# Warm-up products cut shorter at equal columns, and one quad's loads moved along VectorE's queue

## The chip, the cores and the metric

The kernel runs on one core of a Trainium2 chip. The metric is the device time of one execution in microseconds (us). A core has five engines that work side by side, each through its own queue in order: TensorE (PE, with its weight loads shown apart as PEld), VectorE (DVE), ScalarE (ACT), GpSimd (POOL) and SyncE (SP). SyncE only issues transfers here; GpSimd and, at the start, ScalarE issue some too.

## The reference

Attention over 8 batches of 12 heads, 448 positions and 64 dimensions, with q and k normalised first, and then a dense layer with a GELU between two weight matrices.

```
q_n = q / sqrt(mean(q*q) + 1e-6) * g_q          # k likewise with g_k
attn = softmax(q_n @ k_n.T / 8)
x = (attn @ v), heads side by side               # (3584, 768)
out = gelu_tanh(x @ w_in) @ w_out                # w_in (768, 2048), w_out (2048, 768)
```

## The kernel before

**Tiling.** A batch's 12 heads are taken as three quads `c` of four heads. For each quad, q and k are loaded (`load`, line 118, 448 KB each), squared (`square`), summed (`total`), turned into inverse roots (`rsqrt`), multiplied (`normed`) and transposed, so that positions lie along the free axis. Scores are made in 21 units per batch (three quads by seven tiles of positions, `unit`, line 327), each 128 by 896; ScalarE takes the exponential of each (`exp`, line 338) out of one of a few PSUM buffers. `products` (line 369) multiplies the exponentials with ones, for the sums, and with v. The result, divided, is xT (`quad_x`). The first layer (`mm1_turn`, line 521) and the second one (`quartered`, line 473) follow; the second layer of one batch is run in between the attention of the next.

**The order of the work** is written out by hand. Nothing reorders it: what a function emits goes to its engine's queue at that place. Three parts matter.

- The *front*: lines 739 to 896. The first loads go out on SyncE and ScalarE, GpSimd clears and loads the small vectors, and TensorE gets products that nobody reads: `idle(n, w)` (line 266) emits n products of a 128x128 block of ones with 448 columns of ones, into a PSUM tile that is overwritten later. Sixteen stand at the very start (line 802), one ahead of the first scores (line 844), and two at a time behind each of the first five units of batch 0 (the list `mid`, lines 857 to 862). `mid` gives, for each unit's number, what is emitted after its exponential; `first_attention` (line 705) runs it. With only two PSUM buffers for scores here, a unit can't begin before the exponential two units back has read its buffer.
- *Batch 1's attention*: `attention` (line 582) with the tables `SECOND` (line 575). One string gives TensorE's order (steps of the second layer, units, products), another VectorE's: words such as A0, B0, F0, G0 (sums of exponentials), T, R, S (turning and spreading the reciprocals), M (the division into xT). Words L0, L1, K0 and a0 to a5 have no work of their own; each runs the functions that the list `extra` (lines 929 to 948) holds for it, in the order in which they were put in. a0 is there for `total` of batch 2's first quad's q, a1 for its k.
- *Late loads*: `late_loads(b, c)` (line 138) first writes one element of the tile that is to be loaded, on VectorE, and then issues the load on SyncE. The load must wait for that write, so VectorE's place in its queue sets when the transfer is asked for. At L1, behind G0, stand the loads of batch 2's second and third quads, at L0 those of its first. Batch 3's first quad is asked for in the same way ahead of unit 14. The third quad's squares are taken by ScalarE at the end of batch 1's attention (line 675), after the last exponential.

SyncE's queue holds, from batch 1's attention on, loads, stores of results (`store`, line 450) and transfers that transpose (`dma_trans`, line 314), in the order of emission.

Of the kernel before, what the change touches and what calls it, by code (L numbers as in the profile page):

```python
# [17 lines left out]
def kernel(  # L18
# [174 lines left out]
    def rsqrt(b, c=slice(0, NCH), ns=both, near=(), ts=slice(0, NT), twice=False):  # L193

        if b not in rinvs:
            rinvs[b] = smp.tile([P, NCH, 2, 2, NT], F32, tag="rinv", name="rinv")
        lg = smp.tile([P, NCH, 2, 2, NT], F32, tag="lg", name="lg")
        nc.scalar.activation(
            lg[:, c, ns, :, ts], sss[b][:, c, ns, :, ts], AF.Ln, scale=1.0 / D, bias=eps
        )  # L200

        def to_sbuf(far):
            if far:
                ns = slice(far[0], far[-1] + 1)
                nc.scalar.activation(rinvs[b][:, c, ns], lg[:, c, ns], AF.Exp, scale=-0.5)  # L205

        if twice:
            to_sbuf(near)
        if near:
            if ts.start == 0:  # L210
                place(b, c)
            if len(near) == 2:
                t = roots["qk", b, c]
                nc.scalar.activation(t, lg[:, c], AF.Exp, scale=-0.5)
            else:
                t = roots["qk"[near[0]], b, c]
                nc.scalar.activation(t[:, :, ts], lg[:, c, near[0], :, ts], AF.Exp, scale=-0.5)
        to_sbuf([n for n in range(2)[ns] if n not in near])
# [44 lines left out]
                y if i < 2 else dst, z, 1.5, y, op0=ALU.add, op1=ALU.mult  # L263
            )

    def idle(n, w):

        for _ in range(n):
            nc.tensor.matmul(w, filler[:, :128], filler, start=True, stop=True)

    def normed(b, c, n, eng, ts=slice(0, NT)):
        if (n, b, c) not in nrms:
            nrms[n, b, c] = nrmp.tile([P, NT, 2, D], BF16, tag=f"nrm{n}", name=f"nrm{n}")
        m = ts.stop - ts.start
        root = rinvs[b][:, seat(b, c), "qk".index(n)] if eng is nc.gpsimd else roots[n, b, c]
        eng.tensor_mul(  # L276
            nrms[n, b, c][:, ts].rearrange("p t a d -> p a t d"),
            raws[n, b, c][:, :, ts],
            root[:, :, ts].to_broadcast([P, 2, m, D]),
        )  # L280
# [505 lines left out]
    def warm():  # L786
        return oall[0][:, :S]
# [11 lines left out]
    for h in range(2):  # L799
        nc.gpsimd.tensor_mul(gprod[h * D:(h + 1) * D], grow[:, 0], grow[:, 1])  # L800
    nc.gpsimd.tensor_mul(gbf, grow[:, 0], grow[:, 1])
    idle(16, warm())
    for a in range(2):
        square(0, 0, "q", nc.scalar, slice(a, a + 1))
        total(0, 0, "q", slice(a, a + 1))
# [47 lines left out]
    def turn_new(c, ts):  # L853
        tps["k"] = ps_m.tile([128, 1024], BF16, tag="mm", name="tp")
        turn(0, c, "k", ts)

    mid = [(0, lambda: idle(2, warm())),
           (1, lambda: turn_new(0, t_rest), lambda: idle(2, warm())),
           (2, lambda: rsqrt(0, 1, near=(0, 1)), lambda: idle(2, warm())),
           (3, lambda: put(0, 0, "k", t_rest), lambda: normed(0, 1, "q", nc.vector),  # L860
            lambda: normed(0, 1, "k", nc.vector, t_first), lambda: idle(2, warm())),
           (4, lambda: idle(2, warm())),
           (5, lambda: turn(0, 1, "q"), lambda: put(0, 1, "q"),
            lambda: turn_new(1, t_first), lambda: put(0, 1, "k", t_first)),
           (6, lambda: total(0, 2, "q"), lambda: total(0, 2, "k")),
# [50 lines left out]
    for b in range(B):  # L916
        m1, side, extra, ends = [], [], [], []
        if b == 0:

            m1 = [(0, lambda: total(1, 0, "k"),  # L920
                   lambda: total(1, 2, "q"), lambda: total(1, 2, "k"),
                   lambda: rsqrt_newton(1), lambda: normed_both(1, 2, nc.gpsimd),
                   lambda: normed(1, 0, "k", nc.gpsimd)),
                  (2, lambda: total(1, 1, "q"), lambda: total(1, 1, "k"),
                   lambda: normed(1, 0, "q", nc.vector), lambda: rsqrt_last(1),
                   lambda: normed_both(1, 1, nc.vector)),
                  (6, lambda: trans(1, 0, nc.scalar), lambda: late_transposed(1, 2)),
                  (7, lambda: trans(1, 1))]
            extra += [("L0", lambda: late_loads(2, 0)),
                      ("L1", lambda: late_loads(2, 1), lambda: late_loads(2, 2)),  # L930
                      ("K0", lambda: gain(1, 2))]

            for n in "qk":
                sqs[n, 2, 1] = [
                    nrmp.tile([P, NT, 2, D], BF16, tag=f"nrm{m}", name="sq")
                    .rearrange("p t a d -> p (t a d)").bitcast(F32)
                    .rearrange("p (a t d) -> p a t d", a=1, t=NT) for m in "qk"
                ]

            extra.append(("K0", lambda: gpsimd_waits(kT[:1, 2, 0, 0, :1])))  # L940
            at = 0
            for c in range(2):
                for n in "qk":
                    for hs in (slice(0, 1), slice(1, 2)) if c else (both,):
                        extra += [
                            ("K0", lambda c=c, n=n, hs=hs: square(2, c, n, nc.gpsimd, hs)),
                            (f"a{at}", lambda c=c, n=n, hs=hs: total(2, c, n, hs))]
                        at += 1
        elif b + 1 < B:

            m1.append((0, lambda: gpsimd_waits(ess[b, NCH - 1][:1, 0, 0, :1])))
            for c in range(NCH):
                if b == 1 and c + 1 == NCH:
                    m1 += [(0, lambda: total(2, 2, "q")), (0, lambda: total(2, 2, "k")),
                           (0, lambda: rsqrt_last(2))]
                m1 += [(0, lambda c=c: normed_both(b + 1, c, nc.gpsimd)),
                       (4 * c + 4, lambda c=c: transposed(b + 1, c))]
            m1 += [(9, lambda: gain(b + 1, 0)), (14, lambda: gain(b + 1, 1))]
        if 0 < b and b + 2 < B:
            m1 += [(4, lambda: loads(b + 2, 1)), (8, lambda: loads(b + 2, 2))]  # L960
            for c, at in ((0, 4), (1, 9)):
                for i, (n, a) in enumerate((n, a) for n in "qk" for a in range(2)):
                    m1.append((at + i, lambda c=c, n=n, a=a: squared(b + 2, c, n, a)))
                m1 += [(at + 2, lambda c=c: total(b + 2, c, "q")),
                       (at + 4, lambda c=c: total(b + 2, c, "k"))]
            for n in "qk":
                m1.append((13, lambda n=n: square(b + 2, 2, n, nc.gpsimd)))
                extra.append(("first", lambda n=n: total(b + 2, 2, n)))
        if 0 < b and b + 1 < B:
            extra.append(("first", lambda: gain(b + 1, 2)))  # L970
        m1 = plan(*m1)
        for f in range(nf // 2 if b == 0 else nf):
            i, part = f // 4 * 2, f % 4
            if b == 0:
                if f == 2:
                    mm1(0, 5)
                    square(1, 1, "k", nc.scalar)
                elif f > 2:
                    mm1_pair(f)
            elif f == 1:  # L980
                mm1_turn(b, 0, 1, late)
                mm1_turn(b, 1, 1, late)
                mm1_turn(b, 0, 0, late, end=True)
            elif f == 3:
                mm1_turn(b, 1, 0, late, end=True)
            elif part == 1:
                mm1_turn(b, i, 0, range(HP), begin=True)
                mm1_turn(b, i + 1, 0, range(HP), begin=True)
                mm1_turn(b, i, 1, range(HP), end=True)
            elif part == 3:  # L990
                mm1_turn(b, i + 1, 1, range(HP), end=True)
            for fn in m1.get(f, ()):
                fn()
        if b + 1 == B:
            final(b)
            break
        nc.scalar.preload_act_table_set(EXP_SET)
        if b + 2 < B:
            ends.append(lambda: rsqrt(b + 2, slice(0, NCH if b else NCH - 1)))
            side += [(0 if b else 11, lambda: load_v(b + 2, 0, HP))]  # L1000
            if b + 3 < B:
                side.append((3, lambda: loads(b + 3, 0)) if b else (14, lambda: late_loads(3, 0)))
        if b == 0:
            start.close()
            ps_x = ctx.enter_context(
                tc.tile_pool(name="ps_x", bufs=1, space=bass.MemoryType.PSUM))
            for i in (2, 3):
                rounds.append(ps_x.tile([128, 2, 512], F32, tag=f"t{i}", name=f"t{i}"))
            late_on.append(b)
        attention(b + 1, plan(*side), plan(*extra), ends)  # L1010
# [30 lines left out]
```

## Time and profile before

| | |
|---|---|
| median of the 3 runs | 393.74 us (393.16 to 394.86) |
| the profiled execution | 391.3 us |
| its span, first to last instruction | 389.4 us |
| mean granted clock of TensorE | 0.999 |
| TensorE busy | 381.8 us |
| ScalarE, VectorE, GpSimd busy | 278.9, 237.2, 125.2 us |

The profile is of one execution. In a timeline row stand the start, the time that the instructions merged into it cover, the engine (a q behind it means its queue, where a transfer is issued), the line of the kernel, the operation with what it writes and reads, how many there are, and in brackets how long the engine had stood still before and what ended that. The chain that ended last is followed back from the last instruction, at each step to what released it. A matmul's shown time holds its latency; how far apart two begin says what one costs in a stream.

### The profile page before, as it was taken

The page shows a single profiled execution, that of the slowest core. Times are in us where ns is not written, and L with a number is a line of the kernel's source. Part 1 is how long each engine was busy: PE and PEld are TensorE (multiplying, and loading weights), DVE is VectorE, ACT ScalarE, POOL GpSimd, SP SyncE. Part 2 cuts the span into 40 slices and gives each one's busy share as a digit, 9 for nine tenths or more (in the row PEclk, how much of TensorE's full clock was granted, in tenths as well). Part 3 has the DMA queues.
Part 4 walks back from the last instruction along what each step waited for, and adds up shares of the span by engine and source line. Part 5 has one row for each costly group of instructions (what it writes and reads, how often), then busy time and mean ns, then how long its engine had stood idle before and what let it go on. Part 6 is the DMA issues. An engine that isn't in the chain of part 4 may idle for free.

```text
span 389.4 us, 17468 instructions
## 1 busy us (share of the span) xinstructions
PE 381.8 (98%) x8023; PEld 290.6 (75%) x8023; DVE 237.2 (61%) x367; ACT 278.9 (72%) x353; POOL 125.2 (32%) x107
## 2 busy tenths in 40 slices
PE   8899999999999999999999999999999999999996
PEld 3365567777887788877888778877888778887664
DVE  5998937976596259836589256953598304980010
ACT  6995499767994689757996589946897449944300
POOL 5995505484005440083102740064400900000000
PEclk9999999999999999999999999999999999999999
DMA  8999999999714992369722995159622831120033
GB/s 276 319 229 210 210 153 346 217 191 247 133 44 98 247 206 60 82 128 265 149 66 67 177 260 107 44 115 246 108 63 65 128 40 44 44 65 4 2 81 83
DMA packets 64414, 54.68 MB, mean 140 GB/s; under 512 B 37588, under 2 KB 59988, under 8 KB 64340
## 3 DMA queue, kind: packets, MB, share of 16 engines
q1 hardware_dynamic: 53904, 41.33, 46.0%
q0 software_dynamic: 10128, 11.80, 18.4%
q8 instruction: 63, 1.03, 1.1%
q10 hardware_dynamic: 308, 0.43, 0.3%
q14 instruction: 11, 0.09, 0.1%
HBM read 45.61 MB, written 11.01 MB: 145 GB/s over the span
## 4 chain that ended last, share of the span: by engine, by line
PE 92%; ACT 4%; DMA 1%; POOL 1%; SPq 0%; DVE 0%; issue 0%; DVEq 0%
PE t L535 33%; PE t L493 32%; PE t L385 9%; PE t L333 7%; PE t L461 5%; PE t L554 4%; ACT ex L341 4%; DMA rawq<-in_q_dram 1%; POOL g L164 1%; PE h L434 1%; PE tp L294 0%; PE o L385 0%; SPq L743 0%; PE os L385 0%; DVE ss L173 0%
## 5 line engine op out<-in xcount | busy, mean ns | idle before, releaser
L341 ACT ACTIVATE ex<-t,shift 128x896 bf16<-128x896 f32 x168 | 156.3, 1013 | 1.8 <-PE t L333 1.6
L493 PE MATMUL t<-wout,g 64*64 64x384 bf16 (+1 forms) x3456 | 151.8, 305 | 0.2
L493 PEld LDWEIGHTS <-g 64*64 64x64 bf16 x3456 | 113.9, 107 | 20.1 <-issue 1.2
L535 PE MATMUL t<-xT,win 64*64 64x448 bf16 x2688 | 128.6, 349 | 0.0
L535 PEld LDWEIGHTS <-win 64*64 64x64 bf16 x2688 | 96.1, 107 | 31.1
L541 ACT ACTIVATE g<-t 128x896 bf16<-128x896 f32 x56 | 50.5, 915 | 57.1 <-PE t L535 57.1
L173 DVE TENSOR_REDUCE ss<-sq 128x14 f32<-128x896 f32 (+3 forms) x45 | 44.6, 997 | 52.7 <-ACT sq L162 49.0
L333 PE MATMUL t<-qT,kT 64*64 64x448 bf16 x672 | 59.5, 351 | 1.9 <-ACT ex L341 0.8
L353 DVE TENSOR_TENSOR es<-ex 128x1792 bf16<-128x1792 bf16 x20 | 21.2, 1059 | 32.8 <-ACT ex L341 32.8
L276 POOL TENSOR_TENSOR nrmq<-rawq,rinv 128x896 bf16<-128x896 f32 (+1 forms) x21 | 34.7, 1652 | 15.9 <-ACT rinv L205 12.0
L791 POOL COPY mark<-es 1x1 bf16<-1x1 bf16 x6 | 1.1, 177 | 117.6 <-DVE es L360 113.4
L276 POOL TENSOR_TENSOR nrmk<-rawk,rinv 128x896 bf16<-128x896 f32 x20 | 33.7, 1689 | 0.0
L333 PEld LDWEIGHTS <-kT 64*64 64x64 bf16 x672 | 26.0, 106 | 9.2 <-issue 2.5
L385 PE MATMUL t<-ex,vb 64*64 64x448 bf16 x588 | 32.0, 350 | 0.0
L395 DVE STREAM_TRANSPOSE st<-t 128x448 f32<-128x448 f32 x42 | 24.7, 627 | 9.6 <-PE t L385 9.6
L385 PEld LDWEIGHTS <-vb 64*64 64x64 bf16 x672 | 23.5, 107 | 7.1 <-issue 1.0
L407 DVE STREAM_TRANSPOSE rb<-rc 128x896 f32<-128x896 f32 (+1 forms) x25 | 26.7, 1067 | 0.3
L699 DVE COPY osb<-t 128x384 f32<-128x384 f32 (+1 forms) x4 | 2.0, 507 | 35.2 <-PE t L461 35.2
L420 DVE TENSOR_TENSOR xT<-t,rb 128x896 bf16<-128x896 f32 x21 | 22.8, 1086 | 0.8
L511 ACT COPY osb<-t 128x768 f32<-128x768 f32 (+1 forms) x18 | 12.6, 702 | 14.0 <-PE t L493 14.0
L164 POOL TENSOR_TENSOR sq<-rawq 128x896 f32<-128x896 f32 (+1 forms) x9 | 13.6, 1512 | 27.4 <-DVE ss L173 27.4
L356 DVE TENSOR_TENSOR es<-es,ex 128x1792 bf16<-128x1792 bf16 x20 | 21.2, 1062 | 0.7 <-ACT ex L341 0.7
(103 smaller groups left out, 313.4 us busy)
## 6 DMA issues: line engine op xcount, KB each, us to landing
rawq<-in_q_dram SPq DMA_DIRECT2D x23, 448.0 KB, 5.0
rawk<-in_k_dram SPq DMA_DIRECT2D x23, 448.0 KB, 5.6
out_dram<-osb SPq DMA_DIRECT2D x42, 192.0 KB, 2.7
vb<-in_v_dram POOLq DMA_DIRECT2D x6, 672.0 KB, 7.7
win<-in_moe_w_in_dram POOLq DMA_DIRECT2D x8, 384.0 KB, 10.8
wout<-in_moe_w_out_dram POOLq DMA_DIRECT2D x3, 768.0 KB, 18.3
out_dram<-osb SPq DMA_DIRECT2D x24, 96.0 KB, 2.9
vb<-in_v_dram POOLq DMA_DIRECT2D x2, 448.0 KB, 15.5
```

What stands on the lines that cost most here:

```text
L173: nc.vector.reduce_sum(sss[b][:, seat(b, c), "qk".index(n), hs, ts], squares(b, c, n, hs, ts), axis=AX.X)
L276: eng.tensor_mul(nrms[n, b, c][:, ts].rearrange("p t a d -> p a t d"), raws[n, b, c][:, :, ts], root[:, :, ts].to_broadcast([P, 2, m, D]),)
L333: nc.tensor.matmul(sc[r * R:(r + 1) * R, a, :S], kT[rs, c, t, r], qT[b][rs, c, :, r], start=True, stop=True,)
L341: nc.scalar.activation(exs[b, c][:, t], scs.pop((b, c, t))[:, :, :S], AF.Exp, scale=scale, bias=shift)
L353: nc.vector.tensor_add(es, ex[:, :2], ex[:, 2:4])
L385: nc.tensor.matmul(o[r][a * D:(a + 1) * D], vb[b % 2][rs, 2 * c + a, i] if what else ones[rs], es[i][rs, a], start=(i == 0), stop=(i == n ...
L395: nc.vector.transpose(st[:, r].rearrange("p a b -> p (a b)"), o[r])
L407: nc.vector.transpose(oas["rb"][:, rs].rearrange("p r s -> p (r s)"), rc.to_broadcast([128, (rs.stop - rs.start) * m, 32]),)
L420: nc.vector.tensor_mul(xT[b][:, 2 * c:2 * c + 2], oas["o", c, 1][:, :, :S], oas["rb"])
L493: mm = nc.tensor.matmul(o[a * R:(a + 1) * R, bank, :hi - lo], g[rs, f, at:at + R], wout[rs, f, lo:hi], start=(n == 0), stop=(n == len(step ...
L535: mm = nc.tensor.matmul(h[a * R:(a + 1) * R, j, :S], win[rs, c, at:at + R], xT[b][rs, c], start=begin and c == cs[0], stop=end and c == cs ...
L541: nc.scalar.activation(g[:, 2 * i:2 * i + 2, (b % 2) * S:(b % 2 + 1) * S], h[:, :, :S], AF.Gelu_apprx_tanh,)
```

## The change

`idle` gets a third argument, the number of columns. The start's 16 products of 448 columns become 28 of 256; the pairs of 448 behind the first five units become groups of seven of 128 columns; the single one of line 844 stays. In batch 1's attention the third quad's loads of batch 2 move from the word L1 to the word a1.

```
-    def idle(n, w):
+    def idle(n, w, cols=S):
         for _ in range(n):
-            nc.tensor.matmul(w, filler[:, :128], filler, start=True, stop=True)
+            nc.tensor.matmul(
+                w[:, :cols], filler[:, :128], filler[:, :cols], start=True, stop=True
+            )
...
-    idle(16, warm())
+    idle(28, warm(), 256)
...
-    mid = [(0, lambda: idle(2, warm())),
-           (1, lambda: turn_new(0, t_rest), lambda: idle(2, warm())),
-           (2, lambda: rsqrt(0, 1, near=(0, 1)), lambda: idle(2, warm())),
+    mid = [(0, lambda: idle(7, warm(), 128)),
+           (1, lambda: turn_new(0, t_rest), lambda: idle(7, warm(), 128)),
+           (2, lambda: rsqrt(0, 1, near=(0, 1)), lambda: idle(7, warm(), 128)),
            (3, lambda: put(0, 0, "k", t_rest), lambda: normed(0, 1, "q", nc.vector),
-            lambda: normed(0, 1, "k", nc.vector, t_first), lambda: idle(2, warm())),
-           (4, lambda: idle(2, warm())),
+            lambda: normed(0, 1, "k", nc.vector, t_first), lambda: idle(7, warm(), 128)),
+           (4, lambda: idle(7, warm(), 128)),
...
-            extra += [("L0", lambda: late_loads(2, 0)),
-                      ("L1", lambda: late_loads(2, 1), lambda: late_loads(2, 2)),
+            extra += [("L0", lambda: late_loads(2, 0)), ("L1", lambda: late_loads(2, 1)),
+                      ("a1", lambda: late_loads(2, 2)),
                       ("K0", lambda: gain(1, 2))]
```

Instruction by instruction, the orders of ScalarE, GpSimd and SyncE are those of before. On VectorE the two markers of the third quad's loads stand at another place. TensorE has 37 more pairs of weight load and product.

## Prediction

> **What bounds the kernel now.** I began with the page's totals and its chain that ended last.
>
> ```profile
> span 389.4 us, 17468 instructions
> PE 381.8 (98%) x8023; PEld 290.6 (75%) x8023; DVE 237.2 (61%) x367; ACT 278.9 (72%) x353; POOL 125.2 (32%) x107
> PE 92%; ACT 4%; DMA 1%; POOL 1%; SPq 0%; DVE 0%; issue 0%; DVEq 0%
> ```
>
> TensorE is busy for 98% of the span and makes 92% of the chain. Busy time alone doesn't prove that it is at its pace, so I went on to the chain in order of time, where the stretches that belong to other engines show.
>
> ```profile
> 2.18 5.57 DMA rawq<-in_q_dram
> 7.82 3.47 POOL g L164 x3
> 12.52 5.42 ACT ex L341 x6
> 18.49 9.13 ACT ex L341 x10
> 28.05 0.38 PE os L385 x8
> 76.52 18.22 PE t L535 x384
> ```
>
> The columns are start, length and what ran. Up to 18.49 + 9.13 = 27.62 us the end is set by a load, GpSimd's squares and then sixteen exponentials on ScalarE. From there on it is TensorE. So an edit of the front pays only if that first chain ends at another time, and an edit of batch 1's attention (50 to 76 us) pays only by closing or opening gaps of TensorE. The stretches say how many gaps there are (columns: length, busy time of PE, PEld, DVE, ACT, POOL, granted clock, DMA share, GB/s):
>
> ```profile
> 12.00:14.00 2.00, 1.37 (x14) 0.63 (x15) 1.71 (x3) 1.97 (x4) 1.98 (x2) 1.00 1.06 382
> 16.00:20.00 4.00, 3.37 (x65) 1.97 (x57) 3.98 (x8) 3.97 (x8) 3.98 (x6) 1.00 1.18 259
> 50.00:60.00 10.00, 9.88 (x233) 6.73 (x234) 4.51 (x12) 9.97 (x13) 0.00 (x0) 1.00 1.27 170
> 60.00:76.00 16.00, 15.94 (x366) 12.15 (x362) 14.35 (x23) 13.61 (x19) 8.03 (x9) 1.00 0.98 290
> ```
>
> Between 50 and 76 us TensorE stands still for 0.12 + 0.06 = 0.18 us. That is all that the second edit could win there. The front has gaps on TensorE (0.63 us in 12 to 14), but ScalarE is full.
>
> **The 16 products at the start become 28.** Columns: 16 x 448 = 7168, and 28 x 256 = 7168.
>
> ```profile
> 0.78 5.82 PE L269 MATMUL o<-const-bfloat16-1.0 128*128 128x448 bf16 x16 [0.78 <-PEq L1025]
> 1.11 0.15 PEld L269 LDWEIGHTS <-const-bfloat16-1.0 128*128 128x128 bf16 x1 [0.22 <-issue]
> 5.96 0.15 PEld L269 LDWEIGHTS <-const-bfloat16-1.0 128*128 128x128 bf16 x1 [0.22 <-issue]
> 6.97 0.19 PE L829 MATMUL t<-gbf,rows 32*128 32x32 bf16 x2 [0.37 <-DVE nrmq L276]
> ```
>
> Weight loads come at 1.11 and, 13 steps on, at 5.96: 4.85 / 13 = 0.373 us per product, 0.83 ns per column. That is nearly twice the 0.20 us of later ones (below), though the granted clock is shown as 1.00 throughout: the slow start has to be read from spacings. At 0.83 ns a product of 256 columns takes 0.213 us, longer than its weight load of 0.15 us, and 28 of them take 5.97 us, as 16 x 0.373 = 5.97 do. **Zero.** No row has 256 columns at the slow pace. From below, the weight load alone (0.15 us) bounds it: 4.2 us, a gain of 1.8 us on TensorE that nobody can use, since the next product waits for VectorE until 6.97. From above, a price per product instead of per column (0.373 us) gives 10.4 us. I take the price per column.
>
> What hides a small excess: the fillers end at 6.60 and TensorE then waits 0.37 us. Behind that, ScalarE's first three exponentials leave 0.17 us before the logarithm at 11.97, which waits for VectorE:
>
> ```profile
> 8.99 2.81 ACT L341 ACTIVATE ex<-t,shift 128x896 bf16<-128x896 f32 x3
> 11.97 0.32 ACT L198 ACTIVATE lg<-ss,eps 128x28 f32<-128x28 f32 x1 [0.18 <-DVE ss L173]
> 12.46 5.48 ACT L341 ACTIVATE ex<-t,shift 128x896 bf16<-128x896 f32 x6
> ```
>
> So up to 0.37 + 0.17 = 0.54 us costs nothing, 0.019 us per product; above 0.23 us per product each further one shows in the end.
>
> **The five pairs between scores become five groups of seven.** 2 x 448 = 7 x 128 = 896 columns.
>
> ```profile
> 7.94 0.35 PE L269 MATMUL o<-const-bfloat16-1.0 128*128 128x448 bf16 x1
> 10.32 0.38 PE L333 MATMUL t<-qT,kT 64*64 64x448 bf16 x4
> 10.64 0.55 PE L269 MATMUL o<-const-bfloat16-1.0 128*128 128x448 bf16 x2
> 13.50 0.38 PE L333 MATMUL t<-qT,kT 64*64 64x448 bf16 x4 [0.31 <-ACT ex L341]
> 21.03 0.56 PE L294 MATMUL tp<-ident,nrmq 128*128 128x128 bf16 x7
> 21.84 0.34 PE L294 MATMUL tp<-ident,nrmk 128*128 128x128 bf16 x3
> ```
>
> One long filler takes 0.35 us from start to end and two take 0.55 us, so a second one adds 0.20 us. Seven transposes have the new groups' exact shape, a 128x128 weight load and 128 columns each: seven in 0.56 us and three in 0.34 us make (0.56 - 0.34) / 4 = 0.055 us apiece. Whole groups stand against each other as 0.56 to 0.55 us. Five groups: **+0.05 us**, and that is covered. The scores that follow a group at 10.32 are done at 10.70 and their exponential can't start before 8.99 + 2/3 x 2.81 = 10.86, a cover of 0.16 us; the other four groups stand before scores that wait for VectorE or for ScalarE anyway, as those at 13.50 do for 0.31 us. If the cover were gone, it would cost those 0.05 us.
>
> The Trainium skill ("TensorE: Matmul & The Clock Gate", section "Back-to-back issue gap") speaks against this shape: it puts a stream of weight load and product of 128 columns at about 81 ns each. By that the groups would take 7 x 0.081 = 0.57 us, 0.19 us more each; the transposes above run at 55 ns, so the trace disagrees.
>
> Together 37 more pairs go through TensorE's queue. The columns streamed are the same.
>
> **The loads of batch 2's third quad move.** The first of their two markers on VectorE now (the second follows at once), and the two instructions between which they will stand:
>
> ```profile
> 59.60 0.06 DVE L142 MEMSET rawq<- 1x1 f32 x1
> 65.52 1.09 DVE L420 TENSOR_TENSOR xT<-t,rb 128x896 bf16<-128x896 f32 x1
> 66.53 1.07 DVE L173 TENSOR_REDUCE ss<-sq 128x14 f32<-128x896 f32 x1
> ```
>
> The step named a1 runs its functions in the order in which they were listed, and the loads are listed ahead of the total. So the markers come *ahead of* VectorE's second total, right behind the multiplication that makes xT: at 65.52 + 1.09 = 66.61 us in place of 59.60, 7.0 us later. Each costs VectorE 0.06 us, as before. SyncE's queue keeps its order:
>
> ```profile
> 61.89 0.42 SPq L124 DMA_DIRECT2D rawq<-in_q_dram  x1
> 63.52 0.37 SPq L124 DMA_DIRECT2D rawk<-in_k_dram  x1
> 66.13 2.51 SPq L454 DMA_DIRECT2D out_dram<-osb  x4
> 68.73 0.54 SPq L124 DMA_DIRECT2D rawq<-in_q_dram  x1
> 75.37 3.22 SPq L454 DMA_DIRECT2D out_dram<-osb  x4
> ```
>
> The two loads go out at about 66.7 and 67.2 us, so the four stores behind them start at 67.6 or so instead of 66.13, and batch 3's first loads at 70.2 instead of 68.73: 1.5 us later each. Who waits for them? Landing times, and ScalarE's users (the first two of this quad, the last of batch 3's):
>
> ```profile
> rawq<-in_q_dram SPq DMA_DIRECT2D x1, 448.0 KB, 6.3
> vb<-in_v_dram POOLq DMA_DIRECT2D x1, 672.0 KB, 9.0
> ```
>
> ```profile
> 77.56 0.95 ACT L162 ACTIVATE sq<-rawq 128x896 f32<-128x896 f32 x1
> 78.41 0.94 ACT L162 ACTIVATE sq<-rawk 128x896 f32<-128x896 f32 x1
> 80.79 1.73 ACT L541 ACTIVATE g<-t 128x896 bf16<-128x896 f32 x2 [1.45 <-PE t L535]
> 82.41 0.58 ACT L162 ACTIVATE sq<-rawq 128x448 f32<-128x448 f32 x1
> ```
>
> This quad's load took 6.3 us to land. In the new place it meets the stores, batch 3's loads and the load of v, so I price it between 6.3 and the 9.0 us of that larger load: q lands at 73.0 to 75.7 us, k at 73.5 to 76.2. The squares start at 77.56 and 78.41, so at least 1.9 us are left. Batch 3's, asked for at 70.2, land by 79.2, and are used at 82.41. In the program each issue of SyncE also waits until the one eight before it has landed: k's landing at 76.2 would hold the second of the four stores at 75.37 for 0.5 us or so, and with it batch 2's transposes behind, whose scores come after TensorE's 76.52 + 18.22 = 94.74. For the earlier stores nothing waits but the reuse of their buffers. **Zero**; if the cover were gone, ScalarE has another 1.45 us of idle time behind the squares before TensorE could feel it. From below: the second quad's loads, which stay where they are, share the transfers with less, and the gain of that is bounded by TensorE's 0.18 us.
>
> **The sum:** 0.00 at the start + 0.05 covered + 0.00 for the loads, with -0.2 to +0.1 us around it. The profiled execution took 391.3 us, of which 389.4 are its span; the median of the runs shown is 393.74, 2.4 us above, and I carry the same difference: 391.3 + 0.0 + 2.4 = **393.7 us**. The runs shown lie between 393.16 and 394.86, so I give this case 392.6 to 394.9.
>
> **Rivals.** *Faster: the full pace comes earlier.* The runs shown are 1.9 to 3.6 us longer than the profiled one, and no row tells why. If TensorE stays at the slow pace longer in them, and shorter products with more weight loads raise it earlier or hold it, the gain is at most that difference: 2.4 us of the median, 391.3 us. Against it: in the profile the pace is already full at 7.94 us, and the columns per microsecond stay the same. The Trainium skill (same page, section "What's actually happening") lets the clock follow how busy the array was in a free-running window of about 3.4 us, whatever the number of products; by that this rival has nothing to work with, and the sum stays. The spacings above agree with a half clock at the start.
>
> *Slower: the full pace is lost in the front.* Gaps are widest from 12 to 14 us (busy 1.37 of 2.00). If groups of short products count for less, TensorE could fall back to 0.373 us for 448 columns there. From 16 to 20 us it runs 65 products, mostly scores and averages that pass at 0.38 / 8 = 0.048 us each (the row at 28.05): 3.1 us of work in 4.0. At half pace that is 6.2 us, 2.2 us too long, and the exponentials wait for scores behind it: 395.9 us, and 398 for two such stretches. It decides once the slow stretch lasts past 2 us. Against it: the transposes hold the same shape at full pace.
>
> *Slower: short products are paid by count.* At 0.373 us each the first 28 take 10.4 us, 4.6 more than 5.82; less the cover of 0.54 that is 4.1 us: 397.8 us. It begins at 0.23 us per product. Against it is the transposes' 0.055 us.
>
> *The loads are late,* if one takes over 10.9 us to land (66.7 to 77.56); at 14 us ScalarE waits 3.1 us, 1.5 of it uncovered, 395.2 us.
>
> *The edit does nothing that it says* (the markers in fact ahead of the total) costs the same as the forecast and is in it.
>
> **How the numbers follow.** A measurement of this kernel tells about 0.5%, 2.0 us, from no change: under 391.8 is faster, over 395.7 slower. Forecast 0.61; full pace earlier 0.21, nearly all of it at 391.8 or less; pace lost 0.10; paid by count 0.04; late loads 0.04, half of it past the bound. That makes faster 0.20, same 0.64, slower 0.16. The range takes in the faster rival whole, with the scatter of the runs (391.0), and the lower end of the lost pace: 391.0 to 396.2. Left out are the two dear ends, some 0.1.
>
> **What would show it.** In the changed kernel's timeline: the start's fillers end near 6.6 us, weight loads 0.213 us apart; each group of seven takes 0.56 us; the first exponential is at 8.99 and the chain leaves ScalarE at 27.6, all within 0.1 us. The markers stand at 66.6, SyncE's two loads right behind, and ScalarE's squares still at 77.6. If the first exponentials start over 0.5 us later, or the scores from 12 to 28 us show gaps of TensorE that end on TensorE's own work, the forecast of the fillers is wrong; if the squares show a wait for a load, that of the loads; if the front stands still and the time moves by over 2 us, I have mistaken where plain runs differ from the profiled one.

## The result, and the profile after

The changed kernel took 391.0 us in the median of 21 runs (390.45 to 392.88). The kernel before, run beside it 21 times, took 392.7 us (391.32 to 397.83). The ratio is 0.9963, with a 95% interval of 0.9946 to 0.9979: 1.5 us faster by the ratio, and within the 0.5% that was forecast as "same". What changed most is the scatter: 10 of the 21 runs before were above 393 us, none after.

The page of the changed kernel shows nothing of it. Its profiled execution took 391.3 us, as the one before did:

```profile
span 389.5 us, 17541 instructions
PE 381.4 (98%) x8060; PEld 293.4 (75%) x8060; DVE 236.6 (61%) x367; ACT 278.7 (72%) x353; POOL 125.2 (32%) x107
PE 92%; ACT 4%; DMA 2%; POOL 1%; SPq 0%; DVE 0%; issue 0%; DVEq 0%
```

The chain in order of time (start, length, what ran) does. First some landmarks of the changed kernel, then the one of before that the prediction doesn't show:

```profile
2.19 6.26 DMA rawq<-in_q_dram
8.52 3.48 POOL g L164 x3
19.20 9.13 ACT ex L343 x10
50.84 0.61 PE t L495 x12
76.71 18.21 PE t L537 x384
```

```profile
50.15 0.61 PE t L493 x12
```

Two differences cancel. The front ends later, at 28.33 us instead of 27.62, because the load of the second quad's q landed 0.7 us later. From the second layer's first products to the first layer, in batch 1's attention, the changed kernel needs 76.71 - 50.84 = 25.87 us, the one before 76.52 - 50.15 = 26.37. That is 0.5 us out of a stretch in which TensorE seemed to stand still for 0.18 us. TensorE's timeline shows from where; first before, then after:

```profile
56.62 1.45 PE L493 MATMUL t<-wout,g 64*64 64x384 bf16 x20
```

```profile
0.78 5.63 PE L269 MATMUL o<-const-bfloat16-1.0 128*128 128x256 bf16 x28 [0.78 <-PEq L1027]
9.05 0.58 PE L269 MATMUL o<-const-bfloat16-1.0 128*128 128x128 bf16 x7
57.32 0.98 PE L495 MATMUL t<-wout,g 64*64 64x384 bf16 x20
```

The same twenty products of the second layer took 1.45 us before and take 0.98 after. A stop of 0.47 us lay between two of them. It isn't counted as idle, since a product's shown time holds its latency and covers most of the gap.

The loads did what was forecast. On VectorE, SyncE and ScalarE of the changed kernel:

```profile
66.72 0.06 DVE L142 MEMSET rawq<- 1x1 f32 x1
```

```profile
66.83 0.37 SPq L124 DMA_DIRECT2D rawq<-in_q_dram  x1
67.30 1.14 SPq L124 DMA_DIRECT2D rawk<-in_k_dram  x1
68.53 0.47 SPq L456 DMA_DIRECT2D out_dram<-osb  x1
```

```profile
77.75 0.95 ACT L162 ACTIVATE sq<-rawq 128x896 f32<-128x896 f32 x1
```

The marker stands at 66.72 us, the loads go out right behind it, and ScalarE's squares show no wait.

### The profile page after: what moved, and what is told of

Same layout as the page of the kernel before. It is cut to its first block, busy times and chain, and to the rows that moved or that the text cites. A ratio compares the mean times of both kernels' runs of the same rounds, so it can differ in the third digit from the quotient of the medians.

```text
span 389.5 us, 17541 instructions
## 1 busy us (share of the span) xinstructions
PE 381.4 (98%) x8060; PEld 293.4 (75%) x8060; DVE 236.6 (61%) x367; ACT 278.7 (72%) x353; POOL 125.2 (32%) x107
## 3 DMA queue, kind: packets, MB, share of 16 engines
q8 instruction: 63, 1.03, 1.1%
## 4 chain that ended last, share of the span: by engine, by line
PE 92%; ACT 4%; DMA 2%; POOL 1%; SPq 0%; DVE 0%; issue 0%; DVEq 0%
PE t L537 33%; PE t L495 32%; PE t L387 9%; PE t L335 7%; PE t L463 5%; PE t L556 4%; ACT ex L343 4%; DMA rawq<-in_q_dram 2%; POOL g L164 1%; PE h L436 1%; PE tp L296 0%; PE o L387 0%; SPq L745 0%; PE os L387 0%; DVE ss L173 0%; ACT lg L198 0%
## 5 line engine op out<-in xcount | busy, mean ns | idle before, releaser
L495 PEld LDWEIGHTS <-g 64*64 64x64 bf16 x3456 | 112.6, 107 | 19.5
L335 PE MATMUL t<-qT,kT 64*64 64x448 bf16 x672 | 58.1, 351 | 2.3 <-ACT ex L343 0.8
```

What stands on the lines that cost most here:

```text
L335: nc.tensor.matmul(sc[r * R:(r + 1) * R, a, :S], kT[rs, c, t, r], qT[b][rs, c, :, r], start=True, stop=True,)
L495: mm = nc.tensor.matmul(o[a * R:(a + 1) * R, bank, :hi - lo], g[rs, f, at:at + R], wout[rs, f, lo:hi], start=(n == 0), stop=(n == len(step ...
```

## The experiments

**Which part.** Theory F: the fillers' shape raises TensorE's pace earlier or holds it. Theory L: the moved loads free batch 1's attention. Four kernels, each with one part. The first has the new fillers and the old place of the loads:

```
             extra += [("L0", lambda: late_loads(2, 0)),
                       ("L1", lambda: late_loads(2, 1), lambda: late_loads(2, 2)),
```

> The fillers of the changed kernel (28 of 256 columns, groups of seven of 128) with the third quad's loads at their old place L1. If the fillers bring the gain (theory F: they raise TensorE's pace earlier, or hold it, in the runs that are longer than the profiled one), the median falls by the whole 1.5 us or so and the runs above 393 us go. If the loads bring it (theory L), the median stays with the kernel before, within 0.3 us. Under theory L the stretch from the last transposes of batch 1's quad to the first layer (50.15 to 76.52 before, 26.4 us) also stays at 26.4 us, under both the front ends at 27.6 us or as much later as its load lands later.

Measured: 391.38 us (12 runs) beside 393.01 (35 runs of the kernel before, shared by these four); ratio 0.9951, interval 0.9925 to 0.9977. The gain comes with the fillers. The stretch of batch 1's attention took 26.5 us in this trace, no less than the 26.4 before; its execution took 392.07 us, more than the median.

The second has the new place of the loads and `idle(16, warm())`, `idle(2, warm())` as before:

> The kernel before with the third quad's loads at a1 and the old fillers. Theory L: the stretch of batch 1's attention falls from 26.4 to 25.9 us as in the changed kernel, and the median falls by 0.5 us from that, or by the whole 1.5 us if long runs came from this stretch. Theory F: the median stays within 0.3 us, and the 0.5 us in the two profiles is scatter of the transfers.

Measured: 392.59 us, ratio 0.9994, interval 0.9964 to 1.0025. The loads bring nothing that can be measured, and theory L falls. Its trace was the first with a plain stop in it. In TensorE's timeline of this kernel:

```profile
56.53 0.33 PE L495 MATMUL t<-wout,g 64*64 64x384 bf16 x2
58.07 1.00 PE L495 MATMUL t<-wout,g 64*64 64x384 bf16 x18 [1.21 <-issue]
```

Behind two of those twenty products TensorE stops, and what ends the wait is put down to "issue", to nothing that the profile follows. At 0.04 us per product the third should begin at 56.61; it begins at 58.07, 1.46 us later. The stretch from the second layer's first products to the first layer took 27.5 us here.

The third and the fourth have one kind of filler each:

```
-    idle(16, warm())
+    idle(28, warm(), 256)
```

> Only the start's 16 products become 28 of 256 columns. Theory F by the start: the whole of what the fillers bring is here (the pace is raised by the first 6 us). Theory F by the groups, and theory L: same as the kernel before within 0.3 us.

Measured: 391.3 us, ratio 0.9963, interval 0.9936 to 0.999.

```
-    mid = [(0, lambda: idle(2, warm())),
+    mid = [(0, lambda: idle(7, warm(), 128)),
```

and so on for the five.

> Only the five pairs become groups of seven of 128 columns. Theory F by the groups (the pace is held between the scores): the whole of what the fillers bring is here. Theory F by the start, and theory L: same as the kernel before within 0.3 us.

Measured: 391.9 us, ratio 0.9958, interval 0.9929 to 0.9986. Each half alone brings about what both bring. That fits neither form of F, which put all of it in one half.

**A third theory.** What the three good kernels have in common is that TensorE has more instructions ahead of 50 us: 24, 50 and 74 more. The page of before says that instructions come by a transfer queue of their own (packets, MB, share of 16 engines):

```profile
q8 instruction: 63, 1.03, 1.1%
```

63 packets of 16.4 KB make 1.03 MB; TensorE has 2 x 8023 = 16,046 products and weight loads, so 64 bytes each and 256 to a packet. The Trainium skill ("Runtime: NRT & Kernel Launch", section "Instruction fetch mechanics") says the same of the size, that a block is fetched while the one before runs, and that the cost is mostly hidden. Of the 63 refills here, two are seen to stop TensorE for over 0.2 us in the trace of before. The transfers of two stretches, as packets, MB and share of the stretch. Before, 54 to 56 us:

```profile
q1 hardware_dynamic: 439, 0.11, 105.0%
q0 software_dynamic: 111, 0.09, 38.7%
q8 instruction: 1, 0.02, 3.0%
```

After, 50 to 52 us, where the same refill falls now:

```profile
q0 software_dynamic: 358, 0.39, 115.8%
q8 instruction: 1, 0.02, 3.0%
```

Before, the refill shares the engines with 439 packets of some 250 bytes, those of the transposing transfers; after, with larger ones. In the kernel with the loads alone the row of 54 to 56 us reads so:

```profile
q8 instruction: 1, 0.02, 6.4%
```

6.4% of 16 engines in 2 us is 2.05 us for the packet instead of 0.96, and the stop was 1.46 us instead of 0.47. Theory I: the gain comes from where a refill of TensorE's instructions falls.

To move the refill without touching the fillers, products of one column and 32 weights were added:

```
+    def tiny(n):
+        for _ in range(n):
+            nc.tensor.matmul(
+                warm()[:32, :1], filler[:, :32], filler[:, :1], start=True, stop=True
+            )
+    mid += [(i, lambda n=n: tiny(n)) for i, n in enumerate([8, 8, 7, 7, 7])]
```

> The kernel before, its long fillers untouched, with 37 products of a 128x32 weight block and one column spread over the first five units: as many more instructions on TensorE as in the changed kernel (74), and 37 columns in 12096 more. Theory I: the gain comes from where TensorE's instruction stream is refilled. In the kernel before a refill (16 KB, 256 instructions) arrives at about 55 us, while two transposing transfers crowd the queues, and the second layer's products stop for 0.45 us (1.2 us in the run with the loads alone) at the same instruction; 74 instructions more move that refill. By I the median falls by 1.5 us, less what the tiny products cost the front (up to 0.3 us), and the stop at that instruction is gone. Theory F (shape of the fillers, their pace): the median stays at the kernel before's, or above by the front's cost.

Measured: 391.31 us (10 runs, 391.15 to 392.07) beside 392.93 (21 runs); ratio 0.9951, interval 0.993 to 0.9973. The old fillers with 74 instructions more are as fast as the new fillers. In TensorE's timeline the twenty products are whole:

```profile
57.22 0.98 PE L493 MATMUL t<-wout,g 64*64 64x384 bf16 x20
```

With `[18, 18, 18, 18, 18, 19, 19]` instead, 256 instructions more:

> The same with 128 tiny products, 256 instructions, over the first seven units: one whole refill, so that every later refill falls on the same instruction as in the kernel before. By I the stop at the third instruction of the 20 products of the second layer, near 57 us, is back, the median lies 2 us or more above the fastest run, as in the kernel before (393.0 against 390.4), and it isn't faster than the kernel before; the front may cost 0.5 to 2 us on top. By F with weight loads counting for the pace, it is as fast as or faster than the run with 37, but for that cost.

Measured: 394.71 us (393.54 to 395.25), ratio 1.0037, interval 1.0019 to 1.0054. The front cost more than was expected, 2.6 us (the first layer's first products of batch 0 begin at 32.93 us instead of 30.32; with 37 tiny ones at 30.91). Less that, it is 392.1, against 390.7 for the run with 37 less its 0.6, and 392.93 for the kernel before. So more than half of the gain is gone, but not all of it, if the front of this trace is that of the other runs. Theory I had expected a median 2 us or more above the fastest run; it is 1.2. The stop is back at its place, though short in this trace. On the weight loads' timeline:

```profile
59.05 0.11 PEld L493 LDWEIGHTS <-g 64*64 64x64 bf16 x2
59.52 0.62 PEld L493 LDWEIGHTS <-g 64*64 64x64 bf16 x18 [0.36 <-issue]
```

Two more executions of the kernel before, each with its trace:

> The kernel before once more, for a trace of another of its runs (about half are above 393 us). Theory I: the longer the run, the longer the stop near 57 us, with the front unchanged. Theory F: the front is longer, or products pass at half pace somewhere from 7 to 28 us.

> The same again: by theory I what it is longer than the fastest run shows as a stop of TensorE between its own instructions near 57 us, by theory F in the front.

Measured: 391.5 and 392.53 us. Neither was one of the long runs. In both the stop is at the same instruction, 0.45 us in the first and 1.1 us in the second, and each has another of some 0.9 us near 63 us; the stretch took 27.0 and 27.7 us. The second one's timeline:

```profile
56.73 0.33 PE L493 MATMUL t<-wout,g 64*64 64x384 bf16 x2
57.93 1.00 PE L493 MATMUL t<-wout,g 64*64 64x384 bf16 x18 [0.88 <-issue]
```

**Which traffic.** If the transposing transfers hold the refill up, asking for them earlier should help, with TensorE's queue untouched:

```
                   (2, lambda: total(1, 1, "q"), lambda: total(1, 1, "k"),
+                   lambda: late_transposed(1, 2),
                    lambda: normed(1, 0, "q", nc.vector), lambda: rsqrt_last(1),
...
-                  (6, lambda: trans(1, 0, nc.scalar), lambda: late_transposed(1, 2)),
+                  (6, lambda: trans(1, 0, nc.scalar)),
```

> The kernel before with TensorE's queue untouched and the two transposing transfers of batch 1's third quad asked for some 6 us earlier (their markers on VectorE ahead of the first quad's multiplication, not behind the second one's). Theory I says that the refill of TensorE's instructions at 54.5 us is late because it meets these transfers: with them out of the way the stop at the third of 20 products near 57 us shrinks from 0.4 to 1.2 us to under 0.2, and the median falls by 0.7 to 1.5 us with the old fillers. If the refill meets other traffic there (I in a weaker form: only its place counts), the stop and the median stay. Theory F: the median stays.

Measured: 391.79 us (12 runs) beside 393.37 (23 runs); ratio 0.9974, interval 0.9947 to 1.0001: some 1 us less, as theory I with these transfers as the cause expected, but not clear of no change. The premise failed. SyncE issued them 6 us earlier, but they took that much longer (us from issue to landing of k's):

```profile
43.33 5.52 SPq L317 DMA_TRANSPOSE kT<-nrmk  x1
```

```profile
kT<-nrmk SPq DMA_TRANSPOSE x1, 16.5
```

It landed at 59.8 us; before, 9.7 us after an issue at 49.9, at 59.6. The stop was 0.24 us in this trace (the twenty products took 1.22 us), but the next refill's, near 62 us, was 1.2 us, against 0.4 in the trace of before. Whether these transfers are what delays the refill is not settled.

> The changed kernel with the same earlier transposing transfers. If I holds with the transfers as the cause, there is little left to gain, since its refill has already moved: within 0.4 us of the changed kernel (391.0). If they delay later refills too, it is up to 0.5 us faster.

Measured: 391.52 us, ratio 0.9947, interval 0.9923 to 0.997. The median is 0.5 us above the changed kernel's 391.0, the ratio 0.0016 below; the two aren't told apart, so there is no better version in this.

**The changed kernel put back.** The last test keeps all of the change and moves the refill to its old place by 91 tiny products, `[13] * 7`:

> The changed kernel whole, with 91 tiny products (13 behind each of the first seven units): 74 + 182 = 256 instructions more than the kernel before, one refill, so the refills fall where they fell before, with the new fillers and the moved loads in place. By the measured 2.6 us of front for 128 tiny products over 0.6 for 37, 91 cost the front about 1.8 us. Theory I: the stop at the third of 20 products near 59 us is back, and the median lies 0.5 to 1.5 us above the kernel before. Theory F: the fillers keep their gain of 1.5 us, so the median is at 391.0 + 1.8, as much as the kernel before or less, and no stop at that instruction.

Measured: 394.32 us (392.53 to 396.63, 12 runs) beside 392.14 (17 runs); ratio 1.0039, interval 1.0006 to 1.0072. The front cost 2.0 us in its trace, so the rest is 392.3, 2.0 above the changed kernel's 391.0 less its own 0.7 of later front, and no different from the 392.14 of the kernel before. The trace is of a run of 395.6 us and shows the stop at its longest, at the same instruction:

```profile
58.64 0.33 PE L495 MATMUL t<-wout,g 64*64 64x384 bf16 x2
61.49 1.00 PE L495 MATMUL t<-wout,g 64*64 64x384 bf16 x18 [2.53 <-issue]
```

The third product begins 2.77 us later than it should. The refill's packet began between 58 and 59 us; before it began between 54.4 and 54.6. So it came some 4 us later, behind an attention that began 2.0 us later. With the same fillers and the same place of the loads, no gain is left. Theory F in both its forms falls.

**Where the stops stand.** Count TensorE's instructions, weight loads and products together, from the start of each trace. With TensorE's old queue (five traces) the stop among the twenty products stands behind the 1210th; with 256 more (two traces) behind the 1466th. Both numbers are 186 above a multiple of 256. The refills at other places aren't free either. With the new fillers alone, a stop stood further on:

```profile
62.15 0.35 PE L495 MATMUL t<-wout,g 64*64 64x384 bf16 x3 [0.55 <-issue]
```

It is behind the 1466th instruction too, and so are the second stops of 0.4 to 1.2 us that all five traces with the old queue have at 62 to 63 us. With the start's fillers alone, 0.26 us are lost behind the 1210th. So the stops keep their place in the count and not at a product. Behind each of them TensorE went on 1.3 to 1.8 us after a refill's packet had ended.

**What the stops add up to.** In each of the 13 traces, take the time from one product of batch 0 (the same one in all, at 32 to 35 us) to the last product, and subtract TensorE's stops, meaning each spacing of two products that is over 0.2 us longer than in the undisturbed traces. What is left is 352.4 to 352.7 us, whatever the kernel. So these executions differ by their front and by stops, and by nothing else that counts. The kernel put back shows it at its largest: its span is 4.3 us longer than the one before (393.7 and 389.4), 2.0 of it front and 2.3 stops (3.1 and 0.8). Not every stop in these sums is a refill's: one of 1.1 us in the changed kernel with the earlier transfers is behind instruction 2080 and waits for ScalarE.

So the change doesn't remove the wait for instructions. It moves the refills, by the medians to where the wait is shorter on average.

## Why the prediction was right, and where it was wrong

- **The outcome** (same within 0.5%, 391.0 to 396.2) held. Of the 2.7 us between the predicted 393.7 and the measured 391.0, about 1.0 is the sample: three runs of the kernel before had a median of 393.74, 21 had 392.7. The other 1.7 us (1.5 by the ratio) is a real gain, and it was forecast as none. That the outcome held is in part luck: 391.0 is the lowest end of the range, which reached so far down only for a rival whose mechanism is refuted, and it lies under the 391.8 that the prediction itself called faster. Beside the kernel before it is the same only because that one came out 1.0 us lower.
- **The step that failed** is the sentence "37 more pairs go through TensorE's queue. The columns streamed are the same", priced at nothing. The count was what mattered: 74 instructions of old and new kinds alike brought it. With 256, one whole refill, more than half of it was gone with the old fillers and all of it with the new ones, the cost of the front taken off.
- **The bound of 0.18 us** on batch 1's attention was read from idle time and was too small. The stop before was already 0.47 us in the profiled execution and 1.1 us in another. A gap between products shows in where the next one begins, not in the engine's busy time.
- **The price of the fillers** was right: groups of seven took 0.58 us (0.56 forecast), and the 28 ended at 6.41 us (6.60). In other traces the old 16 ended between 5.3 and 6.6 us, so the last 0.2 us mean nothing. The cover held, though only two of the five groups stand before scores that wait (12.32 and 13.50 us before); the others are covered by exponentials that are still running.
- **The front** was forecast to end at 27.6 us within 0.1. It ended at 28.33, because the load of the second quad's q landed later, and not because of the fillers' own time (below). The first exponential began at 9.16 us, not 8.99.
- **The loads** were right: marker at 66.6, measured 66.72; no wait on ScalarE; nothing gained (ratio 0.9994). The stores went out at 68.53 instead of 67.6, which nothing waited for. In the rival of late loads, 3.1 us less 1.45 leave 1.7, not 1.5, so its 395.2 should read 395.4.
- **The rivals.** "The full pace comes earlier" had the sign, and its bound of 2.4 us held, but its mechanism is refuted: the old fillers gained as much with tiny products added, and the new ones lost their gain. In the six traces whose front was read product by product (before, after and the four single parts), scores and products pass at full pace from 8 to 15 us. "Paid by count" was wrong for a product's own time.

Open: the gain itself isn't in the traces. The five with TensorE's old queue have spans of 389.4 to 390.8 us, the six with 24 to 74 instructions more of 389.5 to 390.3: the latter have shorter stops on the whole (0.25 to 1.35 us in sum, against 0.8 to 2.1) and a front that ends about as much later. No trace of the kernel before was of one of its runs above 393 us, where the medians part. That these are long for the same stops is inferred from the size of the stops (0.24 to 2.8 us), from the execution of 395.6 us, and from the scatter that goes when the refill moves; but with 256 instructions on the old fillers the scatter stayed small (393.54 to 395.25). Every kernel with more instructions also has a later front, and none delays the front without adding instructions. So that the stop's place follows the count is shown; that the wait is shorter for the place alone, and not also for the later time, is not.

## What to carry to other kernels

Where a long unrolled kernel keeps one engine full, adding or removing a few instructions early moves every later refill of its instruction stream; here a change of 0.4% went with 74 instructions that do nothing. Before a gain is credited to what was edited, add the same number of idle instructions to the old version, and a whole block of 256, and see whether the gain follows the count. Look for the stop by comparing the length of equal groups of products, not by idle time, and count instructions: here the stop kept its place in the count whatever was added ahead of it.

## What the runs showed of the hardware that was not expected

The refill of instructions shares the transfer engines with data. Its packet of 16 KB took 0.96 us in the trace of before and 2.05 in that of the loads alone, at the same place, and TensorE, which used 256 instructions in about 5.2 us there (64 in 1.30), stopped for 0.24 to 2.8 us.

In the traces of the kernels with more instructions on TensorE, GpSimd could begin the second quad's squares only at 8.10 to 8.80 us; in the five with TensorE's old queue, at 7.43 to 7.92. Before and after, on GpSimd:

```profile
7.82 1.68 POOL L164 TENSOR_TENSOR g<-rawq 128x896 f32<-128x896 f32 x1 [0.39 <-DMA rawq<-in_q_dram]
```

```profile
8.52 1.68 POOL L164 TENSOR_TENSOR g<-rawq 128x896 f32<-128x896 f32 x1 [0.92 <-DMA rawq<-in_q_dram]
```

It cost the front 0.7 us in the changed kernel's trace. It holds even where only products behind the first scores were added, after the load had been asked for, so the number of instructions can't act through TensorE there. Its cause stays open.
